# A fused attention and mixer kernel: one more Strassen-like split in the first row block pair, another order of its parts, and other matmuls at the start

## The chip, the cores and the metric

One core of a Trainium2 chip runs the whole program. The metric is device time in microseconds (us) of one execution, the median of the runs shown. The profile is of one of these executions.

## The reference

Attention in which a query sees only the keys of its hash bucket, and then one block of an MLP mixer:

```python
# q, k, v: (4, 8, 768, 64), proj: (64, 6), all float32
q_bits = (einsum('bhsd,dk->bhsk', q, proj) > 0); k_bits likewise
mask = q_bucket[:, :, :, None] == k_bucket[:, :, None, :]     # bucket: the 6 bits as a number
scores = where(mask, q @ k.T / 8, -1e9)
x = softmax(scores) @ v                                       # -> (4, 768, 512), heads side by side
h = relu(x.T @ w_tok1) @ w_tok2                               # tokens: 768 -> 256 -> 768
u = x + h.T
out = u + relu(u @ w_ch1) @ w_ch2                             # channels: 512 -> 1536 -> 512
```

The change concerns the last line, and the first microseconds of the attention.

## The kernel before, in words

The program has three parts: attention (to 313 us of the profile), tokens (to 387 us) and channels. Every engine's order is the order in which the Python code issues the instructions; nothing reorders them afterwards. A pool hands out named places; a new tile at a place waits until all readers of the old one are done.

`channels` takes the 3072 rows in three stages, s = 0, 1, 2, of a pair of 512-row blocks each. XT holds u transposed; T (halves of TA and TB) holds the four sums of the stage's inputs that a seven-product scheme (Strassen's, in Winograd's form) needs. A stage first makes the hidden layer, which `R` keeps, and then the output (`outputs(s)`: one whole product and six calls of `product`, j = 1 to 6). In stage 0, `hidden(0, t)` does one level of the scheme. In stages 1 and 2 there is a second level: each of the seven products p1 to p7 is itself made of seven smaller ones. `hidden_first(s, 0, ...)` makes the first two of the hidden row blocks in this way, and `hidden_pair(s, t)`, t = 1, 2, the others.

A `Smaller` is one second-level product. Its seven matmuls have 128x128 weights and 256 columns, and go in three groups that other products' groups stand between: `one` (the first, which ScalarE copies away in `keep`), `rest` (three more, after which ScalarE copies the accumulated first quarter in `unite` and VectorE adds it to the others in `add`) and `three`, which accumulate into any bank pair that wants the result; `seed` puts sums back into a bank pair beforehand so that `three` adds to them. Its seven weight blocks are `self.left`: three are raw weights, four are sums of them. For p2, p6, p7, p3 and p4 they come from DRAM (`fetch_hidden_left`, on SyncE's queue), for p5 the sums come from DRAM (`fetch_fifth`), and for p1 they lie in SBUF, made once in stage 0 by `sum_first_left`, for t = 1 and 2 only. The eight right sides are four quarters of the input and four sums of them, which the four VectorE operations of `right_sums(name, s)` (L859 to L862) make.

At t = 0 the kernel before makes p1 otherwise: `opened` (L1036) issues four matmuls of 512 columns, first of all. The list `between` says which right sums are issued at which point inside the block; p5's and p6's are issued before it.

PSUM has four bank pairs in channels, b0 to b3, and `ring` names them in the order of their next use. `hidden_first` calls them X, Z, E and Y. SBUF places are shared likewise: `output_at(0)` to `output_at(3)` hold results of `outputs` (q7, q57 and later q4, q6, q5 and later q2) and then copies of the hidden stage; `left_at(g)` holds the weights of the g-th product of the outputs, and between products right sums.

Stores of outputs (`store`, L1481) are DMAs from GpSimd's queue that add to what lies in DRAM. `look` (L1568, L1576) squares and sums pieces of q and k on ScalarE for a safety test, with a load on GpSimd's queue for each. `residual` writes u to the output in DRAM beforehand.

At the very start (L471) the kernel issues twelve small float32 matmuls of ones on TensorE, whose result nobody reads, while the first inputs come in. `first_hashes` (L325) issues the first matmuls that count.

Of the kernel before, what the change touches and what calls it, by code (L numbers as in the profile page):

```python
# [48 lines left out]
def kernel(  # L49
# [14 lines left out]
    P = 128  # L64
# [193 lines left out]
    def attention(pool, psum, W1, W2, x0):  # L258
# [213 lines left out]
        for _ in range(12):  # L472
            nc.tensor.matmul(idle[:D, :D], ones, ones, start=True, stop=True)  # L473
# [281 lines left out]
    def channels(pool, psum, SW1, second, TA, judge):  # L755
# [135 lines left out]
        def first_left_sums():  # L891

            return [
                SW1[:, ::2].rearrange("p i k c -> p i (k c)")[:, :, P * (7 + i) : P * (8 + i)] for i in range(4)
            ]

        def sum_first_left():
            (a00, a01), (a10, a11) = [
                [a[:, 0, P:].rearrange("p (t c) -> p t c", c=P) for a in half]
                for half in weight_quarters(first_weight("p1"))  # L900
            ]
            new = first_left_sums()
            nc.vector.tensor_tensor(new[1], a00, a10, op=ALU.subtract)
            nc.vector.tensor_tensor(new[0], a10, a11, op=ALU.add)
            nc.vector.tensor_tensor(new[2], new[0], a00, op=ALU.subtract)
            nc.vector.tensor_tensor(new[3], a01, new[2], op=ALU.subtract)
# [23 lines left out]
        class Smaller:  # L930


            def __init__(self, h, name, s, t):
                self.h, self.name, self.s, self.t, self.fetched = h, name, s, t, False
                self.b = right_sums(name, s)[1]
                if h is None:
                    raw = [a for b in weight_quarters(first_weight(name)) for a in b]
                    raw = [raw[i][:, 0, P * t : P * t + P] for i in (0, 1, 3)]
                    if name == "p1":
                        sums = [a[:, t - 1] for a in first_left_sums()]  # L940
                    else:
# [26 lines left out]
            def rest(self):  # L968

                self.mm(self.ps[:, 0], 2, 6, False)  # L970
                self.mm(self.ps[:, 1], 0, 4, False)
                self.mm(self.ps[:, 2], 1, 5)
                self.used()
# [57 lines left out]
        def whole(pair, left, right, which, t):  # L1031
            for i in which:
                at = P * (t + GP * i)
                accumulate(pair[:, i], lambda k: left(k)[:, at : at + P], right, range(KC))

        def opened(pair, which, s, t):  # L1036
            start = TT * 2 * s
            whole(pair, lambda k: WC1[:, k], lambda k: XT[:, k, start : start + TT], which, t)

        def open_next(bank, s, t):  # L1040
            p1 = Smaller(None, "p1", s, t + 1)
            p1.pair = bank_pair(bank)
            p1.one(p1.pair, left_at(7 * s + 1)[:, 2 * TT : 4 * TT])
# [13 lines left out]
        def hidden_first(s, t, between):  # L1057


            r, (p2, p6, p7, p3, p4) = parts_of(s, t)  # L1060
            x, z, e, y = ring
            ring[:] = [y, e, z, x]
            p1, e4, e2, e3 = [flat(output_at(i)) for i in range(4)]
            e7 = flat(q1)
            e5, e6, u = copies(), copies(), copies()
            p5 = Smaller(None, "p5", s, t)
            n = TT * 3 // 2

            X = bank_pair(x)
            opened(X, [0, 1], s, t)  # L1070
            look()
            Z, E = bank_pair(z), bank_pair(e)
            p2.one(E, e2)
            copy_pair(p1, X)
            p2.three(Z, True)
            Y = bank_pair(y)
            p5.one(Y, e5)
            begin_look()
            plus(p1[:, :n], flat(Z)[:, :n], p1[:, :n])
            between[0]()  # L1080
            p2.rest()
            p2.unite()
            end_look()
            p2.add()
            p5.rest()
            p5.unite()
            p5.add(True)
            p6.three(X)
# [3 lines left out]
            p5.seed()  # L1092
            plus(r[0], rows(p1), rows(e2))
            V = bank_pair(e)
            between[1]()
            p7.three(V, True)
            p6.rest()
            p6.finish()
            plus(u, u, e6)
            p7.one(bank_pair(x), e7)  # L1100
            p5.three(Y)
            p5 = e5
            copy_pair(p5, Y)
            p7.rest()
            plus(p5[:, :n], flat(V)[:, :n], p5[:, :n])
            p7.finish()
            p3.one(bank_pair(z), e3)
            p3.three(Y)
            relu(r[0])
            p4.three(V)  # L1110
            p4.one(bank_pair(x), e4)
            p3.rest()
            plus(r[1], banks(Y), rows(u))
            plus(u, u, e7)
            plus(r[2][:, 0], banks(V)[:, 0], rows(u)[:, 0])
            plus(r[2][:, 1, 0], banks(V)[:, 1, 0], rows(u)[:, 1, 0])
            between[2]()
            p3.finish()
# [11 lines left out]
        def hidden_pair(s, t):  # L1130
# [8 lines left out]
            e2, e4, e5, e3 = [flat(output_at(i)) for i in ((0, 2, 2, 0) if t == 1 else (0, 1, 2, 3))]  # L1139
# [97 lines left out]
        ahead, postponed, slots, finished = [], [], {}, [0]  # L1237
# [233 lines left out]
        def outputs(s):  # L1471
# [45 lines left out]
            if s < last:  # L1517
# [9 lines left out]
                    lambda: inputs(s + 1, T, 0), lambda: inputs(s + 1, T, 1),  # L1527
                ])
                add(q4, q4, q7)()
                store(q4, 1, 0)()  # L1530
# [224 lines left out]
```

## Time and profile before

| | us |
|---|---|
| median of 3 runs | 788.62 |
| lowest and highest of them | 788.51, 821.44 |
| the profiled execution's own time | 788.62 |
| its span, first to last instruction | 786.8 |
| TensorE busy (4757 matmul records) | 780.8, 99% |
| VectorE busy | 666.4, 85% |
| ScalarE busy | 481.1, 61% |
| hidden_first of stage 1 on TensorE, start to the start of hidden_pair's first matmul | 524.25 to 546.25 |
| hidden_first of stage 2, the same | 653.04 to 675.03 |

A float32 matmul leaves two records on TensorE. Every matmul of the channels part has the line L783, that of a helper; it is told apart by its time and operands. Times are from the start of the span. "b" is a bank pair in PSUM, "second" the SBUF area of `left_at` and `output_at`, "c" a copy, "WC" and "SW" the weights and sums of w_ch1, "XT", "TA" and "TB" the inputs. A bracket at the end of a line gives how long the engine had been idle before it and what ended that.

### The profile page before, as it was taken

To read this page: it belongs to the slowest core of one execution; us is meant where nothing else is said; L and a number is where in the kernel's file an instruction comes from. 1 tells how busy PE (TensorE), PEld (TensorE's weight loads), DVE (VectorE), ACT (ScalarE), POOL (GpSimd) and SP (SyncE) were. 2 spreads that over 40 slices of the span, in tenths; PEclk is the share of its full clock that TensorE was granted. 3 is DMA by queue.
4 is the path that set the end of the run, shared out by engine and by line. 5 is a ranking of instruction groups with operands and counts; after the bars stand their busy time and mean duration, and the time that the engine had idled before them with its cause. 6 is when DMAs were issued, how large, how long until landed. Compare 5 with 4: busy or idle time off the path is not lost.

```text
span 786.8 us, 12638 instructions
## 1 busy us (share of the span) xinstructions
PE 780.8 (99%) x4757; PEld 483.0 (61%) x4757; DVE 666.4 (85%) x910; ACT 481.1 (61%) x831; POOL 53.5 (7%) x77
## 2 busy tenths in 40 slices
PE   9999999999999999999999999999999999999997
PEld 5444444444444444455544448888887887886886
DVE  5989898989887677999787889889899798889884
ACT  6688888888888887333323225655784666665331
POOL 1000000000000000011121010120000122000001
PEclk9999999999999999999999999999999999999999
DMA  4435353537352425796596997797766687650565
GB/s 165 164 123 164 124 164 124 164 123 244 124 171 91 132 86 174 201 264 135 101 278 222 297 376 276 231 284 203 238 218 210 245 242 184 189 170 1 187 167 133
DMA packets 102530, 145.40 MB, mean 185 GB/s; under 512 B 30200, under 2 KB 72640, under 8 KB 102464
## 3 DMA queue, kind: packets, MB, share of 16 engines
q1 hardware_dynamic: 94448, 119.68, 46.4%
q0 software_dynamic: 7728, 24.64, 13.6%
q8 instruction: 39, 0.64, 0.3%
q14 instruction: 27, 0.22, 0.1%
q10 hardware_dynamic: 288, 0.21, 0.1%
HBM read 101.53 MB, written 35.52 MB: 174 GB/s over the span
## 4 chain that ended last, share of the span: by engine, by line
PE 99%; DVE 0%; issue 0%; DVEq 0%
PE b L783 50%; PE sc L356 20%; PE acc L410 16%; PE t L656 5%; PE t L696 5%; PE sums L434 2%; PE hp L301 1%; PE idle L473 0%; PE hw L325 0%; DVE second L1023 0%; DVE ones L97 0%; PE b L1598 0%; DVEq L1750 0%
## 5 line engine op out<-in xcount | busy, mean ns | idle before, releaser
L363 ACT ACTIVATE e<-sc 128x768 f32<-128x768 f32 x192 | 154.5, 810 | 6.6 <-PE sc L356 6.2
L356 PE MATMUL sc<-qk 64*128 64x384 f32 x768 | 153.3, 485 | 0.0
L783 PE MATMUL b<-R,second 128*128 128x256 f32 (+1 forms) x522 | 131.9, 409 | 0.0
L410 PE MATMUL acc<-e,vn 128*32 128x384 f32 x1536 | 127.0, 486 | 0.0
L783 PEld LDWEIGHTS b<-R,second 128*128 128x128 f32 x522 | 99.0, 190 | 28.7 <-issue 16.5
L395 DVE TENSOR_TENSOR esd<-esd,e 128x768 f32<-128x768 f32 x96 | 92.0, 958 | 10.4 <-ACT e L363 0.5
L410 PEld LDWEIGHTS acc<-e,vn 128*32 128x32 f32 x1536 | 49.9, 110 | 73.9 <-issue 73.5
L356 PEld LDWEIGHTS sc<-qk 64*128 64x128 f32 x768 | 68.5, 188 | 42.3 <-issue 38.1
L789 ACT COPY c<-b 128x256 f32<-128x256 f32 (+1 forms) x96 | 40.2, 425 | 79.4 <-PE b L783 68.9
L783 PE MATMUL b<-XT,WC 128*128 128x256 f32 (+1 forms) x212 | 65.0, 444 | 0.0
L356 PE MATMUL sc<-bits 64*128 64x384 bf16 x384 | 62.5, 323 | 0.0
L783 PEld LDWEIGHTS b<-XT,WC 128*128 128x128 f32 x212 | 40.1, 190 | 19.2 <-issue 14.9
L391 DVE SCALAR_TENSOR_TENSOR esd<-e 128x768 f32<-128x768 f32 x32 | 30.6, 955 | 23.4 <-ACT e L363 23.4
L783 PE MATMUL b<-XT,SW 128*128 128x256 f32 (+1 forms) x164 | 46.7, 410 | 0.0
L656 PE MATMUL t<-x,W 128*128 128x512 f32 x96 | 41.8, 593 | 0.0
L356 PEld LDWEIGHTS <-bits 64*128 64x128 bf16 x384 | 18.6, 94 | 32.9 <-issue 9.6
L783 PEld LDWEIGHTS b<-XT,SW 128*128 128x128 f32 x164 | 31.1, 190 | 9.4 <-issue 4.1
L416 ACT ACTIVATE num<-acc,vsum 128x384 f32<-128x384 f32 x32 | 18.6, 581 | 29.8 <-PE acc L410 29.4
L716 POOL DMA_DIRECT2D XT<-second x8 | 9.9, 1234 | 383.5 <-DVE second L715 355.8
L455 ACT COPY rec<-rec 32x384 f32<-32x384 f32 x64 | 32.6, 510 | 5.0 <-DVE rec L449 4.2
L398 DVE TENSOR_TENSOR esd<-esd,e 128x768 f32<-128x768 f32 x32 | 30.5, 954 | 1.9
L656 PEld LDWEIGHTS t<-x,W 128*128 128x128 f32 x96 | 18.2, 190 | 22.7 <-issue 21.3
(255 smaller groups left out, 1272.3 us busy)
## 6 DMA issues: line engine op xcount, KB each, us to landing
second<-left SPq DMA_DIRECT2D x20, 768.0 KB
raw<-in_moe_w_ch SPq DMA_DIRECT2D x16, 768.0 KB
qk<-in_qk SPq DMA_DIRECT2D x15, 768.0 KB
second<-left SPq DMA_DIRECT2D x18, 576.0 KB
seen<-in_qk POOLq DMA_DIRECT2D x21, 384.0 KB, 5.5
WC<-hidden_left SPq DMA_DIRECT2D x18, 448.0 KB
vn<-in_v SPq DMA_DIRECT2D x16, 384.0 KB
vt<-in_vT SPq DMA_DIRECT2D x16, 384.0 KB
```

The costliest lines, as they stand in the source:

```text
L356: nc.tensor.matmul(sc[:, i, :HALF], t[rows, 1, P * c : P * c + P], t[rows, 0, qs], start=start, stop=not start,)
L363: nc.scalar.activation(e, sc[:, :, :HALF], ACT.Exp, scale=SCALE)
L391: nc.vector.scalar_tensor_tensor(self.d, es[0], NR * EPS, es[1], op0=ALU.add, op1=ALU.add,)
L395: nc.vector.tensor_tensor(self.d, self.d, e, op=ALU.add)
L398: nc.vector.tensor_tensor(self.d, self.d, self.es[-1], op=ALU.add)
L410: nc.tensor.matmul(acc[D * i + d : D * i + d + 32], vn[:, i, c, d : d + 32], e[:, i], start=(c == 0), stop=(c == NR - 1),)
L416: nc.scalar.activation(nums[self.n][:, self.half], acc, ACT.Identity, scale=-1.0, bias=vsum,)
L455: nc.scalar.copy(rec[other : other + 32, h], rec[at : at + 32, h])
L656: nc.tensor.matmul(ps, W1[:, r, P * j : P * j + P], x[:, r], start=(r == 0), stop=(r == NR - 1),)
L696: nc.tensor.matmul(ps[at], left, right, start=start, stop=True, skip_group_check=True,)
L783: nc.tensor.matmul(ps, left(k), right(k), start=start and k == ks[0], stop=stop and k == ks[-1], skip_group_check=True,)
L789: nc.scalar.copy(c, ps)
```

## The change

It makes p1 at t = 0 of seven smaller products as well. For that, `sum_first_left` makes the four weight sums for t = 0 too, at places of their own, and `hidden_first` gets another order of its parts: p2.one, p1.one and p2.three come first; p1 gets keep, unite, add, seed and three; the banks' names and the places of p1, e2, e3 and e4 are given out in another way; p5's right sums are issued in the last product of the stage before, p1's, p7's, p6's and p4's inside the block; the last addition of the outputs before (q4) and its store are issued inside the block too; p4.one stands inside p3's rest. `hidden_pair` with t = 1 takes other places. And the twelve float32 matmuls at the start become six bfloat16 matmuls of zeros with 64 weight columns and 384 columns.

```diff
-        for _ in range(12):
-            nc.tensor.matmul(idle[:D, :D], ones, ones, start=True, stop=True)
+        for _ in range(6):
+            zeros = bitrows[0][:, 0]
+            nc.tensor.matmul(idle[:D, :HALF], zeros[:, :D], zeros[:, :HALF], start=True, stop=True)
...
-        def first_left_sums():
+        def first_left_sums(first):
+            if first:
+                tails = [SW1[:, i].rearrange("p k c -> p (k c)")[:, 11 * P : 12 * P] for i in (0, 2)]
+                more = WC1[:, KC:].rearrange("p k c -> p (k c)")[:, 21 * P : 23 * P]
+                return [a.rearrange("p (t c) -> p t c", c=P) for a in (*tails, more[:, :P], more[:, P:])]
...
         def sum_first_left():
-            (a00, a01), (a10, a11) = [
-                [a[:, 0, P:].rearrange("p (t c) -> p t c", c=P) for a in half]
...
+            for first, columns in ((True, slice(0, P)), (False, slice(P, GP * P))):
+                (a00, a01), (a10, a11) = [
+                    [a[:, 0, columns].rearrange("p (t c) -> p t c", c=P) for a in half]
+                    for half in weight_quarters(first_weight("p1"))
+                ]
+                new = first_left_sums(first)
+                nc.vector.tensor_tensor(new[1], a00, a10, op=ALU.subtract)
+                nc.vector.tensor_tensor(new[0], a10, a11, op=ALU.add)
+                nc.vector.tensor_tensor(new[2], new[0], a00, op=ALU.subtract)
+                nc.vector.tensor_tensor(new[3], a01, new[2], op=ALU.subtract)
...
-                        sums = [a[:, t - 1] for a in first_left_sums()]
+                        sums = [a[:, max(t - 1, 0)] for a in first_left_sums(t == 0)]
...
-            def rest(self):
+            def rest(self, between=lambda: None):
                 self.mm(self.ps[:, 0], 2, 6, False)
                 self.mm(self.ps[:, 1], 0, 4, False)
+                between()
                 self.mm(self.ps[:, 2], 1, 5)
                 self.used()
...
+        def first_place(s):
+            return left_at(7 * s + 1)[:, 2 * TT : 4 * TT]
...
         def hidden_first(s, t, between):
             r, (p2, p6, p7, p3, p4) = parts_of(s, t)
-            x, z, e, y = ring
+            e, x, y, z = ring
             ring[:] = [y, e, z, x]
-            p1, e4, e2, e3 = [flat(output_at(i)) for i in range(4)]
+            e3, e4, e2, p1 = [flat(output_at(i)) for i in range(4)]
             e7 = flat(q1)
             e5, e6, u = copies(), copies(), copies()
-            p5 = Smaller(None, "p5", s, t)
+            first, p5 = Smaller(None, "p1", s, t), Smaller(None, "p5", s, t)
             n = TT * 3 // 2
 
-            X = bank_pair(x)
-            opened(X, [0, 1], s, t)
+            X, Z, E, Y = [bank_pair(i) for i in (x, z, e, y)]
+            p2.one(E, e2)
+            first.one(X, first_place(s))
+            between[0]()
+            p2.three(Z, True)
             look()
-            Z, E = bank_pair(z), bank_pair(e)
-            p2.one(E, e2)
-            copy_pair(p1, X)
-            p2.three(Z, True)
-            Y = bank_pair(y)
+            first.rest()
+            first.unite()
+            between[1]()
             p5.one(Y, e5)
-            begin_look()
-            plus(p1[:, :n], flat(Z)[:, :n], p1[:, :n])
-            between[0]()
+            first.add(True)
             p2.rest()
+            first.seed()
             p2.unite()
-            end_look()
             p2.add()
             p5.rest()
             p5.unite()
+            first.three(X)
+            copy_pair(p1, X)
+            between[2]()
             p5.add(True)
+            V = bank_pair(e)
+            p7.three(V, True)
+            plus(p1[:, :n], flat(Z)[:, :n], p1[:, :n])
+            p5.seed()
+            plus(r[0], rows(p1), rows(e2))
+            for work in closing.pop():
+                work()
             p6.three(X)
             p6.one(bank_pair(z), e6, False)
             copy_pair(u, X)
             p6.keep()
-            p5.seed()
-            plus(r[0], rows(p1), rows(e2))
-            V = bank_pair(e)
-            between[1]()
-            p7.three(V, True)
+            p5.three(Y)
+            between[3]()
+            p5 = e5
+            copy_pair(p5, Y)
             p6.rest()
             p6.finish()
+            p7.one(bank_pair(x), e7)
+            look()
+            p3.three(Y)
+            plus(p5[:, :n], flat(V)[:, :n], p5[:, :n])
             plus(u, u, e6)
-            p7.one(bank_pair(x), e7)
-            p5.three(Y)
-            p5 = e5
-            copy_pair(p5, Y)
             p7.rest()
-            plus(p5[:, :n], flat(V)[:, :n], p5[:, :n])
             p7.finish()
             p3.one(bank_pair(z), e3)
-            p3.three(Y)
             relu(r[0])
             p4.three(V)
-            p4.one(bank_pair(x), e4)
-            p3.rest()
             plus(r[1], banks(Y), rows(u))
+            p3.rest(lambda: p4.one(bank_pair(x), e4))
+            p3.unite()
             plus(u, u, e7)
             plus(r[2][:, 0], banks(V)[:, 0], rows(u)[:, 0])
             plus(r[2][:, 1, 0], banks(V)[:, 1, 0], rows(u)[:, 1, 0])
-            between[2]()
-            p3.finish()
+            p3.add()
...
-            e2, e4, e5, e3 = [flat(output_at(i)) for i in ((0, 2, 2, 0) if t == 1 else (0, 1, 2, 3))]
+            e2, e4, e5, e3 = [flat(output_at(i)) for i in ((3, 2, 2, 3) if t == 1 else (0, 1, 2, 3))]
...
-                    lambda: inputs(s + 1, T, 0), lambda: inputs(s + 1, T, 1),
+                    lambda: inputs(s + 1, T, 0), right_sums("p5", s + 1)[0], lambda: inputs(s + 1, T, 1),
                 ])
-                add(q4, q4, q7)()
-                store(q4, 1, 0)()
+                closing.append([add(q4, q4, q7), store(q4, 1, 0)])
...
-            for name in ("p5", "p6"):
-                right_sums(name, s)[0]()
-            hidden_first(s, 0, [right_sums(name, s)[0] for name in ("p7", "p4", "p1")])
+            hidden_first(s, 0, [right_sums(name, s)[0] for name in ("p1", "p7", "p6", "p4")])
```

More of the change, by code (lines that the diff above doesn't have):

```diff
@@ L897, in sum_first_left @@
         def sum_first_left():
-            (a00, a01), (a10, a11) = [
-                [a[:, 0, P:].rearrange("p (t c) -> p t c", c=P) for a in half]
[L900 to L906, printed above, removed]
+            for first, columns in ((True, slice(0, P)), (False, slice(P, GP * P))):
[8 more added lines that the diff above has]
+                nc.vector.tensor_tensor(new[3], a01, new[2], op=ALU.subtract)
         def hidden_left_at(h):
@@ L1029, in relu @@
             nc.scalar.activation(a, a, ACT.Relu)
[L1031 to L1038, printed above, removed]
+        def first_place(s):
+            return left_at(7 * s + 1)[:, 2 * TT : 4 * TT]
         def open_next(bank, s, t):
@@ L1042, in open_next @@
             p1.pair = bank_pair(bank)
-            p1.one(p1.pair, left_at(7 * s + 1)[:, 2 * TT : 4 * TT])
+            p1.one(p1.pair, first_place(s))
             ahead.append(p1)
@@ L1236, in channels @@
         GP = HC // 2
-        ahead, postponed, slots, finished = [], [], {}, [0]
+        ahead, closing, postponed, slots, finished = [], [], [], {}, [0]
         hidden_passed = second["hidden_passed"]
```

## The prediction

> **What bounds the kernel now.** I read the page first (shares, then the chain that ended last), then the stages by windows, then the order in time of TensorE, ScalarE and VectorE around the two places where the changed block starts, then the DMA landings there, and last the first 12 us.
>
> ```profile
> PE 780.8 (99%) x4757; PEld 483.0 (61%) x4757; DVE 666.4 (85%) x910; ACT 481.1 (61%) x831; POOL 53.5 (7%) x77
> ...
> PE 99%; DVE 0%; issue 0%; DVEq 0%
> 524.20:546.20 22.00, 22.00 (x96) 17.86 (x95) 19.89 (x37) 12.99 (x25) 2.36 (x3) 1.00 0.85 218
> ```
>
> The first two lines are the page: TensorE is busy 99% of 786.8 us, and the chain is TensorE alone. The third is the first changed block by windows (TensorE, weight loads, VectorE 19.89, ScalarE 12.99 of 22.00 us). So what TensorE issues less is time saved, unless it then waits; VectorE, at 90% here, is the engine nearest to making it wait.
>
> ```profile
> 524.25 5.32 PE L783 MATMUL b<-XT,WC 128*128 128x512 f32 x16
> 529.41 0.59 PE L783 MATMUL b<-TA,WC 128*128 128x256 f32 x2
> 529.85 1.46 PE L783 MATMUL b<-XT,WC 128*128 128x256 f32 x6
> 531.14 1.46 PE L783 MATMUL b<-second,SW 128*128 128x256 f32 x6
> ...
> 546.25 0.59 PE L783 MATMUL b<-TB,WC 128*128 128x256 f32 x2
> ```
>
> TensorE in order of time (start, us; two records are one matmul). Call 524.25 T: outputs(0) ends and hidden_first begins. The 16 records up to 529.41 are the four 512-wide matmuls of opened and the four 256-wide ones of p2.one and p2.three. From T to the p6.one of the next pair (546.25) there are 4 wide matmuls and 43 narrow ones. Counting a wide one as two, 22.00 us / 51 = 0.4313 us for a 256-wide matmul; nothing between them waits. The second block (653.04 to 675.03) has the same spacing.
>
> ```profile
> 531.34 0.37 ACT L990 COPY second<-b 128x256 f32<-128x256 f32 x1 [0.18 <-PE b L783]
> ...
> 551.59 0.80 ACT L1005 COPY b<-q 128x768 f32<-128x768 f32 x1
> ```
>
> ```profile
> 526.00 0.42 DVE L859 TENSOR_TENSOR second<-TA 128x256 f32<-128x256 f32 x1
> ...
> 533.08 0.68 DVE L995 TENSOR_TENSOR c<-b,second 128x512 f32<-128x512 f32 x1
> 533.80 0.43 DVE L998 TENSOR_TENSOR b<-b,c 128x256 f32<-128x256 f32 x1
> 534.14 1.22 DVE L1023 TENSOR_TENSOR R<-second 128x1024 f32<-128x1024 f32 x1
> ```
>
> Prices: a unite (L990) starts 0.20 us after the end of its whole rest (531.14 to 531.34; 536.75 to 536.95, the rest's third matmul ending at 536.75) and takes 0.37. Four sums (L859 to L862) hold VectorE 1.47 us (526.00 to the next group's 527.47), an add pair (L995, L998) 1.06 (533.08 to 534.14), the 768-wide plus (529.69 before) takes 0.96. A seed (L1005) starts when L998 has written the bank: that one ended at 551.50, the seed began at 551.59; ScalarE is free about 0.72 after a seed starts (estimate from 1024-wide copies, which free it after 0.91).
>
> [...]the stores here, which accumulate, land in 5.9 to 9.9, and these decide.
>
> **The change part by part.**
>
> 1. *p1 in smaller products.* Out: 4 wide matmuls. In: first.one, first.rest, first.three, 7 narrow ones. 8 units become 7: -0.43 us in each of two blocks, -0.86 in all, all on the bound.
>
> 2. *The new work off TensorE.* ScalarE gains keep, unite and seed (0.27 + 0.37 + 0.72 us), VectorE gains first.add (1.06). Times after T: p2.one ends 0.43, first.one 0.86, p2.three 2.16, first.rest 3.45, p5.one 3.88, p2.rest 5.18, p5.rest 6.47, first.three 7.76, p7.three 9.06, p6.three 10.35. First waits: p2.three needs the last plus of product 6 to have read its bank (ended at T + 0.16, now T + 0.45 since the p5 sums stand before it; needed at 0.86). The p1 sums run from 0.37, the third ready at 1.46, needed at 2.16. The p7 sums end near 3.3.
>
> Then the chain that decides: first.rest ends 3.45; unite 3.65 to 4.02; first.add 4.06 to 5.2; seed from 5.29 (first.three needs it at 6.47, it ends 6.1). p2.unite stands behind the seed on ScalarE: 6.02 to 6.39 instead of 5.38. p2.add 6.43, free 7.49; the p6 sums to 8.96; p5.add to 10.02; then plus(p1, Z) ends 10.98. p6.one takes Z's bank and would start at 10.35: it waits to about 11.03, **+0.68**. Queued behind it on TensorE is all the rest. Before, the same plus ended at 530.65 and the bank was wanted at 533.73, so the cover was 3 us. Bounds: 0 (if the seed waits only for L995 and the copies free ScalarE sooner, the chain shortens by about 0.5, and a shorter unite wait takes the rest) to +1.4 (twice; ScalarE's look also late).
>
> 3. *After it.* With that shift, p5.three, p3.three, p4.one and open_next have what they need 0.1 to 1.4 us early. VectorE's order then is r[0] to 12.0, the moved q4 add to 13.2, p4 sums 14.6, p6.add, two pluses to 17.7, p7.add 18.8, r[1] 20.0, u 21.4, r[2] read from V by 22.4. The next pair's p6.one takes V's bank and would start at 22.25: **+0.19** (bounds 0 to 0.5; before it was free 0.94 us early).
>
> 4. *p5 sums into product 6, the q4 add and store into hidden_first.* VectorE idled 1.09 and 0.91 us there before L612, waiting for a store; the p5 sums' 1.47 fill that. Nothing on TensorE (bounds -0.1 to +0.2). The store of q4 moves from 529.81 to about T + 13.4:
>
> ```profile
> 529.81 1.20 POOL L1481 DMA_DIRECT2D out<-second  x1 [5.71 <-DVE XT L862]
> out<-second POOLq DMA_DIRECT2D x1, 512.0 KB, 5.9
> ```
>
> The second line is its landing, 5.9 us after issue. It must have read output_at(1) before p4.one's keep writes there at T + 20.3; the keep has 0.6 us to spare before p4.rest. Free up to a landing of about 7.0 us; other stores took 6.0 to 9.9. I take 0 and keep +0.8 a block as the end. On SP, only hidden-weight loads follow the moved order; those of the first block were issued by 523.2. On POOL the second look's load queues behind the store and isn't wanted in this block.
>
> 5. *The sums for t = 0.* sum_first_left gets four more 128-wide operations, about 0.2 us each (estimate from 0.335 for 256 and 0.87 for 768). VectorE then waited 0.47 us for TensorE at 495.97 and 1.27 for ScalarE at 497.67: nothing.
>
> 6. *The first matmuls.*
>
> ```profile
> L473 PE MATMUL idle<-ones x24: 314/314/369, 1.1 to 3.6; 128*64 128x64 f32 x24
> L325 PE MATMUL hw<-qk,projs x16: 486/678/849, 3.8 to 8.4; 128*32 128x384 f32 x16
> ```
>
> hw starts at 3.85, when its first inputs are in, and runs slow (849 ns) at first, 486 later: the clock isn't released before about 6.9 us, where the scores' passes fall from 0.64 to 0.32. Six bfloat16 matmuls of 384 columns at the slow rate (0.32 each, twice the full-rate pass) run from 1.5, after the memset, to 3.4: before hw's inputs. So 0[...].
>
> **Sum.** Per block -0.43 + 0.68 + 0.19 = +0.44; two blocks +0.88; the rest 0. The profiled execution took 788.62 us (span 786.8), which is the median of the runs shown: 789.5.
>
> **Rivals.**
> - *The waits stay hidden* (787.8): only -0.86 is left. For it: the chain of part 2 has some ten links, and 0.07 us off each removes the wait. Against: two of its links, the whole rest and the seed behind L998, are read from the trace.[...]
> - *The store lands late* (slower than before, 791.1): q4's store takes over 7.0 us, p4.keep waits, p4.rest behind it, with the 8.0 us of the store of 521.48 about 0.8 more in each block on top of the forecast. For it: that one, and 9.9 us at 639.65. Against: DMA is less loaded here (206 GB/s at 540 to 542, against 356 at 520 to 522).
> - [...]
>
> **How the numbers follow.** Forecast 0.50, hidden waits 0.32, late store 0.12, late clock 0.06. The range leaves out the tails of the last two and the early clock: 787.3 to 790.9. No case comes near 2% (15.8 us; about what a measurement of this kernel can tell from no change): within 0.97, faster 0.01, slower 0.02 for what I have not seen.
>
> **What would show it.** Right: no 512-wide matmuls at the head of either block, a hole of about 0.7 us before p6.one ended by VectorE's plus, the blocks 22.0 us long becoming 22.4; p2.unite starting 0.7 us after it could. Wrong: no hole and blocks of 21.6; ScalarE waiting for the store before p4's keep; hw starting elsewhere than 3.85, or slow matmuls past 7 us.

## The result: slower by about half a percent

The changed kernel takes 792.37 us (median of 6 runs, 791.81 to 794.36). The kernel before took 788.53 on the same chip. The ratio is 1.0056 [1.0045, 1.0067]: within 2%, but clear of no change, and above the predicted range of 787.3 to 790.9. One of the six executions of the kernel before took 821.44, in a slower state; a ratio here leaves such executions out and is estimated from all the others, so it differs a little from the quotient of the medians (1.0049 here). The profiled execution took 791.85 us with a span of 790.1, against 788.62 and 786.8.

The page of the changed kernel, its busy times and the chain that ended last:

```profile
PE 780.4 (99%) x4751; PEld 483.0 (61%) x4751; DVE 669.5 (85%) x918; ACT 484.2 (61%) x837; POOL 53.4 (7%) x77
...
PE 71%; issue 22%; POOL 3%; DMA 2%; DVE 1%; SPq 0%; POOLq 0%; ACT 0%; DVEq 0%; ACTq 0%
```

TensorE's busy time hardly moved (780.8 before), but the chain is no longer TensorE alone: a DMA, "out<-second", and GpSimd have come into it. The changed block by windows, first in stage 1 and then in stage 2 (length, then busy us and instructions of TensorE, weight loads, VectorE, ScalarE, GpSimd):

```profile
524.13:548.03 23.90, 22.24 (x101) 18.68 (x100) 21.20 (x39) 14.59 (x28) 2.38 (x3) 1.00 0.80 210
654.62:678.56 23.94, 22.23 (x101) 18.67 (x100) 21.20 (x39) 14.59 (x28) 2.37 (x3) 1.00 0.67 183
```

Each block was 22.0 us long and should have become 21.6 by its matmuls; it is 23.9. Cut at those points, the two profiled executions differ as follows:

| stretch | before | after | difference |
|---|---|---|---|
| start to the first block | 524.25 | 524.13 | -0.12 |
| first block | 22.00 | 23.90 | +1.90 |
| to the second block | 106.79 | 106.59 | -0.20 |
| second block | 21.99 | 23.94 | +1.95 |
| to the last group of products | 101.55 | 101.52 | -0.03 |
| from there to the end | 10.25 | 9.99 | -0.26 |

The sum is +3.24, the whole difference of the spans. So the two blocks explain it. TensorE inside the first of them, in order of time (start, us; two records are one matmul):

```profile
524.13 2.32 PE L784 MATMUL b<-XT,WC 128*128 128x256 f32 x10
...
533.21 1.13 PE L784 MATMUL b<-TB,WC 128*128 128x256 f32 x4
534.18 0.59 PE L784 MATMUL b<-XT,WC 128*128 128x256 f32 x2
535.15 0.70 PE L784 MATMUL b<-TB,WC 128*128 128x256 f32 x2 [0.38 <-DVE second L1030]
535.69 0.59 PE L784 MATMUL b<-TA,WC 128*128 128x256 f32 x2
...
544.76 0.59 PE L784 MATMUL b<-XT,WC 128*128 128x256 f32 x2
546.63 1.56 PE L784 MATMUL b<-XT,SW 128*128 128x256 f32 x6 [1.28 <-ACT second L962]
548.03 0.59 PE L784 MATMUL b<-TB,WC 128*128 128x256 f32 x2
```

The wide matmuls are gone. A matmul is due 0.43 us after the one ahead of it. p6.three (from 533.21) starts just after ScalarE's copy of p1 has ended (533.16) and loses 0.11 at its next step. p6.one was due at 534.61 and starts at 535.15, 0.54 late, held by VectorE's plus. The first matmul of p4.rest was due at 545.19 and starts at 546.63, **1.44 late**, held by ScalarE's p4.keep. After each wait the next step is about 0.11 late again (535.15 to 535.69 is 0.54, not 0.43; 546.63 to 548.03 is 1.40 for three matmuls, not 1.29). Then -0.43 + 0.54 + 0.11 + 1.44 + 0.11 + 0.11 = +1.88, of +1.90 measured. What held the keep, from ScalarE, GpSimd and the DMA view (the last line is the landing after issue):

```profile
546.21 0.37 ACT L962 COPY second<-b 128x256 f32<-128x256 f32 x1 [2.95 <-DMA out<-second]
```

```profile
537.93 1.24 POOL L1489 DMA_DIRECT2D out<-second  x1 [9.65 <-DVE XT L860]
```

```profile
out<-second POOLq DMA_DIRECT2D x1, 512.0 KB, 7.9
```

The keep wants to write e4 into output_at(1), where q4 still lies until its store has landed. The store is issued 13.80 after the block's start and lands at 537.93 + 7.9 = 545.8. Before, it was issued at 529.81 and landed after 5.9. In the second block the landing takes 8.2, and p4.rest is 1.48 late. The keep has less room than before, too: p4.one stood five matmuls ahead of p4.rest and stands three ahead now, so that a keep that waits for nothing ends 0.30 us before p4.rest (e4_elsewhere below) where it ended 1.16 before it. This is that keep in the kernel before, ended at 543.80, with p4.rest at 544.96:

```profile
543.43 0.37 ACT L956 COPY second<-b 128x256 f32<-128x256 f32 x1 [1.69 <-PE b L783]
```

All waits of TensorE for these two causes in the changed kernel:

```profile
PE b L784 <- ACT second L962: 2.6, 2, 1.3
...
PE b L784 <- DVE second L1030: 0.8, 2, 0.4
```

Neither line existed before.

### The profile page after: what moved, and what is told of

It is laid out like the page before. It is cut to its first block, busy times and chain, and to the rows that moved or that the text cites. A ratio compares the mean times of both kernels' runs of the same rounds, so it can differ in the third digit from the quotient of the medians.

```text
span 790.1 us, 12634 instructions
## 1 busy us (share of the span) xinstructions
PE 780.4 (99%) x4751; PEld 483.0 (61%) x4751; DVE 669.5 (85%) x918; ACT 484.2 (61%) x837; POOL 53.4 (7%) x77
## 3 DMA queue, kind: packets, MB, share of 16 engines
q0 software_dynamic: 7728, 24.64, 13.4%
## 4 chain that ended last, share of the span: by engine, by line
PE 71%; issue 22%; POOL 3%; DMA 2%; DVE 1%; SPq 0%; POOLq 0%; ACT 0%; DVEq 0%; ACTq 0%
PE b L784 22%; PE sc L356 20%; PE acc L410 16%; PE t L657 5%; PE t L697 5%; PE sums L434 2%; POOL seen L1593 2%; PE hp L301 1%; DMA out<-second 1%; POOL out L1489 1%; POOL looked L1593 1%; DMA hidden_left<-WC 0%; PE hw L325 0%; PE idle L474 0%; DVE R L833 0%
## 5 line engine op out<-in xcount | busy, mean ns | idle before, releaser
L356 PE MATMUL sc<-qk 64*128 64x384 f32 x768 | 153.1, 484 | 0.0
L356 PEld LDWEIGHTS sc<-qk 64*128 64x128 f32 x768 | 68.4, 188 | 42.1 <-issue 37.8
L356 PE MATMUL sc<-bits 64*128 64x384 bf16 x384 | 62.6, 323 | 0.0
L784 PE MATMUL b<-XT,WC 128*128 128x256 f32 (+1 forms) x208 | 61.0, 428 | 0.0
L356 PEld LDWEIGHTS <-bits 64*128 64x128 bf16 x384 | 18.6, 94 | 33.0 <-issue 9.1
```

The source lines that it names most:

```text
L356: nc.tensor.matmul(sc[:, i, :HALF], t[rows, 1, P * c : P * c + P], t[rows, 0, qs], start=start, stop=not start,)
L784: nc.tensor.matmul(ps, left(k), right(k), start=start and k == ks[0], stop=stop and k == ks[-1], skip_group_check=True,)
```

## The experiments

The theory after the result: most of the loss is p4.keep waiting for q4's store, about 1.44 + 0.11 a block, and the rest p6.one waiting for VectorE's plus. The rivals: the new parts of p1 and the order themselves cost more than they save; the start; the additions that p1 brings. In this section "before" is the kernel before on the same chip. Edits are against the changed kernel unless another is named, and "block" is hidden_first in stages 1 and 2.

**e4_elsewhere: another place for e4**, so that the keep has no store to wait for.

```diff
-            e3, e4, e2, p1 = [flat(output_at(i)) for i in range(4)]
+            e3, e4, e2, p1 = [flat(output_at(i)) for i in (0, 3, 2, 3)]
...
-            e2, e4, e5, e3 = [flat(output_at(i)) for i in ((3, 2, 2, 3) if t == 1 else (0, 1, 2, 3))]
+            e2, e4, e5, e3 = [flat(output_at(i)) for i in ((1, 2, 2, 1) if t == 1 else (0, 1, 2, 3))]
```

> The changed kernel with one difference: e4, which p4's keep writes, goes to output_at(3) (p1's place, read for the last time some 8 us earlier), and hidden_pair with t = 1 uses output_at(1) for e2 and e3. No instruction is moved. Store theory: p4's keep no longer waits for q4's store, each block loses that wait (1.44 us) and the 0.11 us of the restart, so -3.1 us against the changed kernel: about 789.3, blocks of 22.3 to 22.4 us, p6.one's wait unchanged. Rival, that VectorE's and ScalarE's added work is what lengthens the block: the wait shows up at another place, the time stays above 791.

Measured: 789.83 against 788.09, 1.0024 [1.0014, 1.0033], where the change as a whole has 1.0056. The store still took 8.1 us, but the keep starts as soon as its matmul is done, and of TensorE's two causes only the plus is left, with the same 0.8 us in two waits:

```profile
545.04 0.37 ACT L962 COPY second<-b 128x256 f32<-128x256 f32 x1 [1.26 <-PE b L784]
```

So the wait for the store is worth the difference of the two ratios, 0.0032 of 788, some 2.5 us (2.1 by the medians). It is not the whole 3.1 because the next wait then comes out: 0.22 and 0.24 at the next pair's p6.one, for the bank that the prediction's part 3 named. A third hole, 0.27 + 0.1 at p2.three in the first block, stands ahead of the store and can't have been uncovered by this edit. There VectorE, which must first read p2.three's bank, had waited for q3's store:

```profile
522.21 1.22 DVE L613 TENSOR_TENSOR TB<-XT,TA 128x1024 f32<-128x1024 f32 x1 [0.55 <-DMA out<-TB]
```

Five of the profiled executions below have it too (0.13 to 0.31), and that of the changed kernel itself has not.

**p6_sums_earlier: p6's right sums ahead**, so that VectorE's plus comes sooner.

```diff
             first.add(True)
+            between[2]()
             p2.rest()
...
             copy_pair(p1, X)
-            between[2]()
             p5.add(True)
```

> The changed kernel with p6's right sums (1.47 us of VectorE) issued just after first.add, where VectorE sits idle 1.22 us, instead of ahead of p5.add. Bank theory: the plus that reads Z ends near T + 10.0, p6.one no longer waits (-0.75 us a block with its restarts). q4's store is issued about 1.1 us earlier, its wait shrinks to about 1.1. Together some -1.1 us a block: 790.1. If only the store mattered for the end, the bank wait would come back inside the store's wait: 791.5 or more.

Measured: 788.78 against 788.09, 1.0012 [1.0006, 1.0019], blocks of 22.66 and 22.05. p6.one's wait is gone, as expected; more went with it, since q4's addition stands behind the plus on VectorE. Its store is issued 12.84 after the block's start, 0.96 sooner than in the changed kernel, and lands in 7.6 and 7.3, and the keep's wait shrinks from 1.44 to 0.83 in the first block and 0.13 in the second. Here the two suspected costs are one chain, and the larger gain comes through the one that was not touched.

**both: the two together.** Edits as above.

> Both of the former in one: e4 at output_at(3), p6's sums just after first.add. If the two waits are all that the change costs, TensorE has no hole in either block, the blocks take 50 x 0.4313 = 21.6 us, and the time is the kernel before less 0.86 and about 0.1 at the start: 787.5. Rival, VectorE as the bound: a new wait at p4.one, open_next or the next pair's p6.one, 788.5 or more.

Measured: 788.70 against 788.09, 1.0008 [1.0002, 1.0015]. The expected 787.5 was missed. The blocks are 21.95 and 22.24: smaller waits of 0.23 (the bank of part 3) and 0.48 (the next pair's p6 weights) stand in the place of the large ones.

**late_store_alone: the late store in the kernel before.** From the kernel before; its p1 in wide matmuls stays, only q4's addition and store move, with the places of the change.

```diff
-            p1, e4, e2, e3 = [flat(output_at(i)) for i in range(4)]
+            e3, e4, e2, p1 = [flat(output_at(i)) for i in range(4)]
...
             plus(r[0], rows(p1), rows(e2))
+            for work in closing.pop():
+                work()
...
-            e2, e4, e5, e3 = [flat(output_at(i)) for i in ((0, 2, 2, 0) if t == 1 else (0, 1, 2, 3))]
+            e2, e4, e5, e3 = [flat(output_at(i)) for i in ((3, 2, 2, 3) if t == 1 else (0, 1, 2, 3))]
...
-                add(q4, q4, q7)()
-                store(q4, 1, 0)()
+                closing.append([add(q4, q4, q7), store(q4, 1, 0)])
```

> The kernel before (p1 by four wide matmuls, its order of parts) with one thing of the change: q4's last addition and its store issued inside hidden_first, after r[0], and the places of e3, e2, p1 that this needs. Store theory: issue near 536.9; p4's keep is wanted at 543.4 and p4.rest at 544.96; with a landing of 8.2 us as in the changed kernel the block gets 0.7 to 0.8 longer, 790.1 in all; with one of 6.0 nothing, 788.6. Rival, that the split of p1 itself costs the time: 788.6 too, and no wait of ScalarE for a DMA.

Measured: 789.75 against 788.09, 1.0028 [1.0017, 1.0039]. The total lies near the theory's, but the parts do not. The keep does wait for the store (landing 6.9), 2.7 us from the point where ScalarE had nothing else. ScalarE's keep, then TensorE with p4.rest as the last line:

```profile
545.47 0.37 ACT L956 COPY second<-b 128x256 f32<-128x256 f32 x1 [2.74 <-DMA out<-second]
```

```profile
544.17 0.59 PE L783 MATMUL b<-TB,SW 128*128 128x256 f32 x2
544.60 1.46 PE L783 MATMUL b<-XT,SW 128*128 128x256 f32 x6
545.90 0.59 PE L783 MATMUL b<-XT,WC 128*128 128x256 f32 x2
546.33 1.46 PE L783 MATMUL b<-XT,SW 128*128 128x256 f32 x6
```

Yet TensorE lost nothing to that wait: the keep is about 0.67 late and done at 545.84, and p4.rest starts on time, 0.43 after the matmul ahead of it. Here p4.one (544.17) still stands five matmuls ahead. What TensorE lost in this block has other causes. The new place of p1 cost 0.52 + 0.1, since its copy then waits for q2's store. VectorE, later by that and by the moved addition, cost 0.28 + 0.1 at p4.three and 0.4 at the next pair; two steps of 0.24 in between were not traced. The second block kept its 22.00 us, with 0.3 and 0.2 lost after it. So this run shows that moving the addition and its store costs time without the new p1, but it does not measure the keep's wait: that needs p4.one's new place as well.

**closing_earlier: q4's addition and store right after first.add**, six operations sooner.

```diff
             first.add(True)
+            for work in closing.pop():
+                work()
             p2.rest()
...
             plus(r[0], rows(p1), rows(e2))
-            for work in closing.pop():
-                work()
```

> The changed kernel with q4's last addition and its store issued right after first.add, in VectorE's gap of 1.22 us, instead of after r[0]. Store theory: the store is issued some 6 us earlier, near T + 6.8, and lands by T + 15; p4's keep (wanted near T + 20) doesn't wait. The bank wait at p6.one stays (0.75 us a block). As with e4 at another place, the ratio to the kernel before goes from 1.0056 to about 1.002; VectorE is 1.1 us less late at the end of the block, so the 0.2 us that the next pair's p6.one then waited should be gone as well. Rival, a wait that depends on the place and not on the time: no change.

Measured: 789.51 against 788.07, 1.0020 [1.0013, 1.0027]. The store is issued at 530.67, 7.2 after the block's start, and the keep does not wait. The wait of p6.one stays at 0.55 + 0.2, and p2.three waits 0.28 in the first block. The 0.2 at the next pair's p6.one was expected to go and stayed (0.23). The cure of the large wait by time does as much as the cure by place.

**start_alone: the six bfloat16 matmuls in the kernel before.**

```diff
-        for _ in range(12):
-            nc.tensor.matmul(idle[:D, :D], ones, ones, start=True, stop=True)
+        for _ in range(6):
+            zeros = bitrows[0][:, 0]
+            nc.tensor.matmul(idle[:D, :HALF], zeros[:, :D], zeros[:, :HALF], start=True, stop=True)
```

> The kernel before with the six bfloat16 matmuls of zeros at the start and nothing else. By the prediction's step 6: nothing, ratio 1.0000. The profile of the changed kernel had the first block 0.12 us earlier: 0.9998. Rival: the start is what remains between the kernel with both waits removed (1.0008, though its profiled execution was shorter than that of before): the clock is released later on the average, 1.0005 to 1.0008, with a wider spread of the times.

Measured: 788.25 against 788.07, 1.0004 [0.9996, 1.0012]: no effect of the start is resolved.

**both_old_start: both, with the twelve float32 matmuls.** The inverse of that edit, on top of both.

> The changed kernel with e4 at output_at(3), p6's sums after first.add, and the twelve float32 matmuls at the start as before. Rest of the accounts: 0.86 us less of matmuls against 0.8 us of small waits that the profile of the kernel with both still shows (0.2 at the next pair's p6.one in the first block, 0.1 and 0.5 in the second). If the start costs something: ratio 0.9998 to 1.0002; if it costs nothing: 1.0008 again.

Measured: 788.83 against 788.07, 1.0011 [1.0002, 1.0019], where both had 1.0008 [1.0002, 1.0015]. No part of what is left is seen to come from the start.

The next three ask why the store lands so late.

**hold_loads: the loads for p5 and p7 of the next row block after p4.rest.**

```diff
-                if self.fetched and self.name == "p5":
+                if self.fetched and self.t == 0 and self.name in ("p5", "p7"):
+                    held.append(self)
+                elif self.fetched and self.name == "p5":
                     fetch_fifth(self.s, self.t + 1)
...
             p4.finish()
+            while held:
+                held.pop().release()
```

> The changed kernel with two loads of hidden weights (p5's 256 KB and p7's 448 KB for the next pair) issued on SyncE's queue after p4.rest and not in the middle of the block. While q4's store was in flight in the changed kernel (537.9 to 545.9) that queue moved 935 KB and the store took 7.9 us; in the kernel before it moved 221 KB and the store took 5.9. If the loads make the store slow: landing near 7, p4's keep waits about 1 us less a block, ratio 1.003 to 1.0035. If the landing time has another cause: 7.9 again and 1.0056.

Measured: 794.34 against 788.07, 1.0085 [1.0072, 1.0097]. With about half of the bytes on SyncE's queue (0.46 and 0.49 MB) the landings are 7.4 and 8.3, so the keep still waits, 0.95 and 1.52. The held loads now come too late themselves:

```profile
PE b L784 <- ACT second L962: 2.1, 2, 1.4
PE b L784 <- DMA WC<-hidden_left: 2.0, 2, 1.0
```

**no_loads: these loads and p6's left out**, so that the next pair computes with old weights.

```diff
-                if self.fetched and self.name == "p5":
+                if self.fetched and self.t == 0 and self.name in ("p5", "p6", "p7"):
+                    pass
+                elif self.fetched and self.name == "p5":
                     fetch_fifth(self.s, self.t + 1)
```

> The changed kernel without the hidden-weight loads of p5, p6 and p7 in hidden_first (the next pair computes with old weights for these three). SyncE's queue moves nothing while q4's store is in flight. If what SyncE's loads take makes the store land late (held back in part they gave 7.4 and 8.3 us): landing near 6.0 as for the stores that had the engines for themselves, so near T + 19.8, p4's keep doesn't wait, the blocks are 1.5 us shorter, about 789.5 in all. If not: 8 again and 792.

Measured, one execution: 790.36 against 787.78. With nothing on SyncE's queue the store, issued at 538.45 (14.1 after the block's start), lands in 6.1 and 5.9:

```profile
out<-second POOLq DMA_DIRECT2D x1, 512.0 KB, 6.1
```

```profile
545.05 0.37 ACT L962 COPY second<-b 128x256 f32<-128x256 f32 x1 [1.26 <-PE b L784]
```

The keep no longer waits. VectorE's and ScalarE's work beside the store was the same, so the loads of weights beside it are the cause of its late landing. Why half of them, in hold_loads, were nearly as bad stays open.

**late_look: the second look's 384 KB load on GpSimd's own queue later.**

```diff
             p7.one(bank_pair(x), e7)
-            look()
             p3.three(Y)
...
             p4.finish()
+            look()
```

> The changed kernel with the second look (two ScalarE operations and a 384 KB load on GpSimd's queue) moved from after p7.one to after p4.rest. The rival to SyncE's loads: the load on the store's own queue, issued 3.5 us after the store, is served in turn with it. If so the store lands near 6.5 to 7 and the wait shrinks by 1 us; if not, 7.9 to 8.2 as in the changed kernel, and 792.

Measured, one execution: 793.83 against 787.78. The landing stays at 7.9 and 8.3, and p4.rest is 1.10 and 1.51 late:

```profile
546.30 0.37 ACT L962 COPY second<-b 128x256 f32<-128x256 f32 x1 [2.60 <-DMA out<-second]
```

So the load behind the store on the same queue isn't the cause.

**q4_on_gpsimd: q4's addition on GpSimd at the block's head, and its store there.**

```diff
             first.one(X, first_place(s))
+            for work in closing.pop():
+                work()
             between[0]()
...
-                closing.append([add(q4, q4, q7), store(q4, 1, 0)])
+                closing.append([lambda: nc.gpsimd.tensor_tensor(q4, q4, q7, op=ALU.add), store(q4, 1, 0)])
```

> The changed kernel with q4's last addition done by GpSimd and it and its store issued at the head of hidden_first, after first.one. A 512-wide addition took GpSimd 1.3 us, so about 2.5 us; the store is issued near T + 5 (it waits for the store before) and lands by T + 14. Store theory: no wait at p4's keep (-1.55 us a block); VectorE has 1.14 us less to do, so the 0.2 us at the next pair's p6.one does not come; the wait at p6.one (0.75 a block) stays. Ratio 1.0015 to 1.002. Rival: GpSimd's addition slows VectorE's operations beside it, 1.003.

Measured: 793.40 against 787.78, 1.0070 [1.0056, 1.0084]. The store lands in 6.2 and 5.8 and the keep doesn't wait. Instead first.rest waits 1.6 us in each block. GpSimd, VectorE and TensorE in that order:

```profile
525.40 2.65 POOL L1537 TENSOR_TENSOR second<-second 128x1024 f32<-128x1024 f32 x1 [0.82 <-ACT second L790]
...
525.75 2.58 DVE L862 TENSOR_TENSOR second<-XT,second 128x256 f32<-128x256 f32 x1
...
528.48 0.67 PE L784 MATMUL b<-second,WC 128*128 128x256 f32 x2 [1.42 <-DVE second L862]
```

The third of p1's sums took 2.58 us beside GpSimd's addition; the same operation takes 0.42 elsewhere. VectorE's operation ends (528.33) just after GpSimd's (528.05). That the two ran side by side is all that the trace shows of the cause.

**best: GpSimd's addition, earlier p6 sums, p5.one ahead of p2.three, p5's weights loaded after p6.finish, the old start.** It was meant as the version without any of the waits seen by then.

> The changed kernel with each wait that the profiles showed taken away: q4's addition on GpSimd and its store at the head of the block, p6's sums just after first.add, p5.one ahead of p2.three (0.4 us more for the plus that frees Z, which came late by 0.3 to 0.4 when q3's store landed late), the 256 KB load of p5's sums after p6's load, and the twelve matmuls at the start as before. If these are all: two blocks of 21.6 us instead of 22.0, ratio 0.9989 to 0.9992. If more of the block is bound by VectorE or loads: 1.0000 or above.

Measured: 791.82 against 787.78, 1.0050 [1.0036, 1.0064]. It has the same loss at first.rest, 1.19 and 1.16 (VectorE's operation there 2.61 us).

**waits_off: the place and the earlier p6 sums, p5.one ahead of p2.three, p5's weights after p6.finish, the old start**; q4's addition on VectorE as in the change.

> The changed kernel with both waits removed as before (e4 at output_at(3), p6's sums after first.add, the old start), and two small ones more: p5.one ahead of p2.three, so that a late landing of q3's store has 0.43 us more before p2.three wants Z (0.41 us lost in the first block of three profiles), and the 256 KB load of p5's sums behind p6's load (0.5 and 0.8 us lost at the next pair's p6.one in the second block of two profiles). Account of waits: what is left is 0.2 to 0.3 us a block at the next pair's p6.one, behind VectorE: ratio 0.9995 to 0.9998. Rival, that the split costs time which no wait shows: 1.0008 to 1.0011 again.

Measured: 789.32 against 788.10, 1.0016 [1.0008, 1.0024]; missed. The blocks are 22.37 and 22.43. The waits left sum to about 0.8 a block: 0.3 to 0.4 at p7.three, which waits for p2.add, late on VectorE behind the earlier p6 sums; 0.2 at first.three, which waits for its seed; and 0.22 at the next pair's p6.one.

**q4_in_gap: the same, with q4's addition after the p7 sums and e4 back in output_at(1).**

> As waits_off, but q4's last addition stays on VectorE and is issued right after p7's sums, where VectorE sat idle 0.69 us, with the store behind it and e4 back at output_at(1). first.add starts 0.4 us later, first.three then waits about 0.1 us; the store lands before T + 14, long before p4's keep; VectorE is 1.1 us less late at the end, so the next pair's p6.one does not wait. Blocks of 21.7 us instead of 22.0, ratio 0.9991 to 0.9994, faster than both kernels. Rival as there: 1.0008 or more.

Measured: 789.28 against 788.10, 1.0017 [1.0009, 1.0024], blocks of 22.37 and 22.42 with the same waits. The expected gain did not come.

**split_sums: p6's sums in two portions**, three after first.add and the fourth after p1's copy, with e4's other place, the old start, and p5's weights after p6.finish.

```diff
             first.add(True)
+            between[2]((0, 1, 2))
             p2.rest()
...
             copy_pair(p1, X)
-            between[2]()
+            between[2]((3,))
```

> The changed kernel with e4 at output_at(3), the old start, the load of p5's sums behind p6's, p5.one back behind first.rest, and p6's right sums divided: three after first.add (1.1 us, which the gap of 1.22 us holds), the fourth after p2.add. waits_off lost 0.5 us a block where first.three and p7.three start (T + 6.3 to T + 8.1): the whole 1.47 us of sums made p2.add late, and p7.three takes the bank that p2.add reads. If so these waits go, blocks of 21.7 to 22.0 us, ratio 0.9995 to 1.0000. Rival, that VectorE and ScalarE are as full as they can be: the loss turns up at another part, 1.0008 or more.

Measured: 788.50 against 787.94, 1.0008 [0.9999, 1.0016]: not told apart from the kernel before. Its blocks by windows, and TensorE at the end of the first:

```profile
523.52:545.45 21.93, 21.87 (x102) 18.69 (x100) 20.25 (x38) 14.88 (x29) 2.38 (x3) 1.00 0.77 197
652.10:674.02 21.92, 21.87 (x101) 18.67 (x100) 20.24 (x38) 14.88 (x29) 2.37 (x3) 1.00 0.61 163
```

```profile
543.93 1.46 PE L783 MATMUL b<-XT,SW 128*128 128x256 f32 x6
545.45 0.67 PE L783 MATMUL b<-TB,WC 128*128 128x256 f32 x2
```

The large waits are gone, yet of the 0.43 that a block should save only 0.07 is left. What remains is mostly one wait: the next pair's p6.one was due at 545.23 and starts at 545.45, **0.22 late**, after VectorE's last read of the bank of part 3 (it ends at 545.34). The second block has the same 0.22, and p6.three loses 0.1 in each. The profiled execution took 787.87, the lowest of its 13 and 0.6 below their median. Its start is enough for that: the first matmuls, 849 ns long at their slowest in the kernel before (the prediction's part 6), are nearly all fast here,

```profile
L325 PE MATMUL hw<-qk,projs x16: 486/498/636, 3.8 to 7.6; 128*32 128x384 f32 x16
```

and its first block begins at 523.52, 0.73 before that of the kernel before, with the same twelve matmuls ahead. No version beat the kernel before.

## Why the prediction was wrong, point by point

- *Part 1, -0.43 a block*: held; it is seen as soon as the waits are taken off (21.92 us in split_sums with its 0.22 and 0.1, against 22.00).
- *Part 2, +0.68 for p6.one*: held, chain and all. first.add starts at T + 4.06, the seed at T + 5.30, p2.unite at T + 6.03, the plus that frees Z at T + 10.02, and p6.one at T + 11.02. The wait was 0.54 and not 0.68 because p6.one was itself due 0.13 later, mostly by p6.three's 0.11; with the 0.11 after it, it is 0.65.
- *Part 3, +0.19 for V's bank*: in the changed kernel itself the larger wait of p4.rest covers it. Without that (e4_elsewhere) it was 0.22 and 0.24.
- *Part 4, "Free up to a landing of about 7.0 us" and "I take 0"*: **this step failed.** It cost 1.44 + 0.11 a block, 3.1 us in two, against a result that lies 2.9 above the forecast. ScalarE waiting for the store before p4's keep is the sign that the prediction had named. Two terms of it were too small. The store was issued at T + 13.80, not 13.4, because q4's addition ended at T + 13.37 instead of 13.2 and GpSimd issued 0.43 after that instead of 0.2. The landing was 7.9 and 8.2, not below 7.0. In the first block 0.37 us more passed between the landing and the keep; in the second that was 0.08. The landing decides: with the 5.9 us of the old place the store would have landed at T + 19.7, and the keep could start as late as about T + 20.6 without holding p4.rest. The "0.6 us to spare" was too much as well: the keep ends 0.30 before p4.rest when nothing holds it.
- *The rival with the late store* had the right mechanism and 0.12 of the chance. Its price, 0.8 a block, was about half of the measured 1.55: the landing was about the 8.0 that it took, and the issue's 0.4 and the 0.11 after the wait were not in it.
- *Why the landing was misjudged.* The argument against this rival was the DMA rate of one stretch, 206 GB/s. What mattered, as no_loads shows, is whether SyncE's queue moves loads while the store runs, and the trace of before already held that number. This is the kernel before, in the stretch where the moved store would run (537.65 to 545.55; packets, MB, share of 16 engines):

```profile
q1 hardware_dynamic: 2446, 1.23, 54.9%
q0 software_dynamic: 49, 0.20, 6.3%
```

  q1 carries SyncE's loads (the three loads issued in that stretch, 448, 448 and 256 KB, are all SyncE's): 1.23 MB. Around the early store, from 529.81 to 535.7, it carried 0.23. In the same trace two stores of the same size and kind show what this does: that of 649.90 with nothing on q1 landed in 5.9, that of 631.26 in 8.1 with 0.92 MB beside it (631.26 to 639.36):

```profile
q1 hardware_dynamic: 173, 0.92, 37.2%
out<-second POOLq DMA_DIRECT2D x1, 512.0 KB, 8.1
```

  By those two the landing would have been read as about 8, which is the case that the prediction itself priced at 0.8 us a block.
- *Part 5*: held. The four operations took 0.28 to 0.29 us each and no matmul waited.
- *Part 6, 0 for the first matmuls*: held. The six run 0.32 us apart, from 1.50 to 3.63, hw starts at 3.75 instead of 3.85, and start_alone shows no effect. What the part took for fixed is not: in the 17 profiled executions, one of each kernel, the trace's record of the granted clock starts, at full clock, between 4.1 us (split_sums) and 7.8 (q4_on_gpsimd), from 4.1 to 6.9 with the twelve matmuls and from 4.4 to 7.8 with the six. In the kernel before it starts at 6.93 and in the changed one at 6.49, and around that time the scores' passes (L356) go from 0.80 us apart to 0.32. What sets the time was not shown; the late clock, with its 0.06, and the early clock were the author's estimates. So a profiled execution can be some tenths of a microsecond faster or slower by its start alone, and the blocks are compared by their own lengths.
- *The rest of the sum*: without the store's wait (e4_elsewhere) the change measured +1.74 in the medians, where the forecast said +0.88. The holes that were not foreseen are 0.27 + 0.1 at p2.three in the first block, where part 4 had put nothing, and the 0.1 to 0.2 a wait that TensorE loses beside it; what else lies in that difference was not separated.

## What to carry to other kernels

When a store moves, its landing need not be the one that it had at the old place (5.9 us there and 7.9 and 8.2 at the new one here): look, in the stretch where it will run, at what the other DMA queues move there, and price it by a store of the same kind that has that beside it. Ask who waits for the buffer that it reads; a different place for the next tile of that buffer was here worth 2.1 to 2.5 us. And count how many matmuls lie between the buffer's next writer and what TensorE needs of it: a keep that came 0.67 us late cost nothing with five matmuls' distance, and with three it had 0.30 us of room. When a chain on a second engine is cut to fit by tenths of a microsecond, removing its largest wait can bring out the next (0.22 and 0.24 us in e4_elsewhere), so the gain in the matmul count (0.43 a block) is worth having only with a margin on that engine.

## What the runs showed of the hardware

- **An accumulating store of 512 KB landed in 5.8 to 6.3 us with no loads on SyncE's queue beside it, and later, 5.9 to 9.4 us, with 0.41 MB of them or more.** These are the 119 stores from output places in stages 0 to 2 of all 17 kernels, by what SyncE's queue moved while each ran:

| MB on SyncE's queue | stores | landing, us |
|---|---|---|
| 0 to 0.01 | 23 | 5.8 to 6.3 |
| 0.23 to 0.30 | 3 | 5.9 to 6.3 |
| 0.41 to 0.51 | 8 | 5.9 to 8.9 |
| 0.59 to 0.80 | 8 | 6.6 to 7.6 |
| 0.81 to 1.16 | 45 | 6.5 to 9.4 |
| 1.21 to 1.58 | 32 | 7.3 to 8.7 |

  It isn't a proportion: a store that runs longer has more loads counted beside it, closing_earlier's two stores, with 0.45 MB each, took 7.1 and 5.9, and what spreads the lower rows was not separated. A 384 KB load on the store's own queue made no difference in late_look (7.9 and 8.3 without it, 7.9 and 8.2 with it).
- **After a wait TensorE lost about another 0.1 us** at the next step in these traces: 0.54 instead of 0.43 at 535.15, and 1.40 instead of 1.29 at 546.63; 0.07 to 0.11 in the other runs.
- **Beside a GpSimd addition of 128x1024 on SBUF, one VectorE operation on SBUF took 2.58 us (q4_on_gpsimd, the addition 2.65) and 2.61 us (best, the addition 2.35)** instead of 0.42, in the first block. The loss at first.rest that follows it was there in both blocks: 1.6 us each in q4_on_gpsimd, 1.19 and 1.16 in best.
